# Raw weight pieces loaded across stages, and q and k loaded five steps ahead in place of nine

## The chip, the core and the metric

The kernel runs on one core of a Trainium2 chip. The metric is the device time of one execution in microseconds (us); the time of a kernel is the median of several runs.

## The reference

Talking-heads attention on 8 batches of 12 heads, 448 positions and 64 dimensions, followed by a Fourier mix and a feed-forward layer. Everything is float32 except the two weight matrices, which come as float64.

```python
scores = scale * np.matmul(q, k.transpose(0, 1, 3, 2))
scores = np.einsum('bhij,hg->bgij', scores, w_pre)      # mix the heads
scores = scores - np.max(scores, axis=-1, keepdims=True)
attn = np.exp(scores)
attn = attn / (np.sum(attn, axis=-1, keepdims=True) + 1e-09)
attn = np.einsum('bhij,hg->bgij', attn, w_post)         # mix them again
x = np.matmul(attn, v)                                  # -> (8, 448, 768)
# ...
X = np.fft.fft(np.fft.fft(x, axis=1), axis=2)
u = x + np.real(X)
un = (u - mu) / np.sqrt(var + 1e-06)
out = u + np.maximum(un @ w_ch1, 0.0) @ w_ch2
```

## The kernel before

It has two phases. The mix phase does attention and the Fourier mix and stores u; the feed-forward phase reads u back and multiplies by both weight matrices in a scheme with seven products for eight. The mix phase is a software pipeline of 192 steps, 24 for each batch (`GS = 24`, `TOT = 192`). The order of instructions on TensorE (PE), VectorE (DVE), ScalarE (ACT) and GpSimd (POOL) is fixed by the program; each engine works its list in order. One step is this:

```python
while s < TOT or any(fill.values()):
    old = len(later)
    n = take("none", s)                  # loads that are due: q, k, v
    if 0 <= s + LM < TOT:
        emit_premix(s + LM)              # PE L449, LM = 2 steps ahead
    flush()
    if 0 <= s < TOT:
        emit_postmix(s)                  # PE L486, needs the scaled PP of step s
    if 0 <= s + LM < TOT:
        emit_max(s + LM)                 # DVE L457
        emit_exp(s + LM)                 # ACT L465
    take("AV", s)                        # PE L513
    if 0 <= s < TOT:
        emit_turn(s)                     # DVE L497, one a step
    if s >= 4:
        wts.deal(1)                      # one DVE operation of the weights' work
    take("QK", s)                        # PE L423
    # ... gather of step s + 4 on SP (Kr <- Sb)
    if 0 <= s + LM < TOT:
        emit_scale(s + LM)               # POOL L476, two instructions
    for _ in range(old):
        later.pop(0)()
    for _ in range(min(len(folds), 1 if n and s > 3 else 2)):
        folds.pop(0)()                   # POOL L567 to L588
    take("full", s)                      # transposes (L400, L546), emit_z (L611), emit_s2 (L627)
    s += 1
```

q and k of the next batch come in six tiles, in the order k0, q0, q2, k1, q1, k2; each is loaded in two halves, in two steps, with two DMAs that POOL issues (batch 0's are issued by SP and ACT). There are four buffers for them. The tile is transposed at its step `a`, and its load is due nine steps before, unless the buffer rule (`old`) puts it later:

```python
old = loads[-4] + 2 if len(loads) > 3 else -99
loads.append(f + a - GS)
for y in range(2):
    due("none", max(old, f + a - GS - 9) + y,
        lambda b=b, xx=xx, nm=nm, y=y: emit_load_qk(b, xx, nm, y))
# ...
for pr in range(3):
    due("none", f + AT_AV[-1][pr] + 2, lambda b=b, pr=pr: emit_load_v(b, pr))
```

The Fourier mix along the positions works on folded operands. A pair of row groups brings 8 folds on POOL, and the second pair of a batch 4 more (`both`, L588), which write `xf`, the operand of TensorE's L611. emit_z takes whatever folds are still open:

```python
def emit_z(b, par, y):
    while ("xf", par) not in batches[b] or folds:
        folds.pop(0)()
    # ... 4 matmuls on st["xf", par] (L611)
```

The weights' work turns the float64 matrices into float32 tiles and their sums, on DVE, between the other work. A stage is four raw pieces of 7 DVE operations each, then four sums, then a store; in the mix phase there are five stages, dealt one DVE operation a step from step 4 on, and 25 more in the feed-forward phase. There one stage is added at a time, and ended before the next block (`wts.deal(1000)`).

```python
def add(self, c, n):
    ps, sums, w, dst = self._parts(c)[n]
    raws, box = {}, {}

    def load(k):
        if k < len(ps):
            src, f, _ = ps[k]
            raws[k] = self.praw.tile([P, DH, 2], U32, name="raw64", tag="raw64")
            nc.gpsimd.dma_start(out=raws[k][:, :f, :].rearrange("p f w -> p (f w)"),
                                in_=src.bitcast(U32))

    def begin(k):
        # ...
        load(k + self.ahead)             # ahead = 1 in the mix phase, 2 after it
        raw = raws.pop(k)
        # ...
        vec.tensor_scalar(box["tmp"].bitcast(U32), box["hi"], 0x7fffffff, None,
                          op0=ALU.bitwise_and)     # L218
    # ...
    self.ops.append((lambda: [load(k) for k in range(self.ahead)], False))
```

Of the kernel before, what the change touches and what calls it, by code (L numbers as in the profile page):

```python
# [11 lines left out]
U32 = mybir.dt.uint32  # L12
# [4 lines left out]
P = 128  # L17
# [20 lines left out]
GS = NG * GT  # L38
# [24 lines left out]
DH = DM // 2  # L63
# [68 lines left out]
def _f32(bits: int) -> float:  # L132
    return float(np.array(bits, np.uint32).view(np.float32))
# [11 lines left out]
class _Weights:  # L145
# [7 lines left out]
    def __init__(self, nc, w_ch1, w_ch2, scr):  # L153
        self.nc = nc
        self.w_ch1, self.w_ch2 = w_ch1, w_ch2
        self.w1 = [scr.tile([7, P, NK, FC], F32, name=f"w1_{c}") for c in range(NC)]
        self.w2 = [scr.tile([7, P, FM, DH], F32, name=f"w2_{c}") for c in range(NC)]
        self.ops = []

    def open(self, ctx, tc, ahead=1):  # L160
        self.ahead = ahead
# [29 lines left out]
    def add(self, c, n):  # L191

        nc, vec = self.nc, self.nc.vector
        ps, sums, w, dst = self._parts(c)[n]
        raws, box = {}, {}

        def load(k):
            if k < len(ps):
                src, f, _ = ps[k]
                raws[k] = self.praw.tile([P, DH, 2], U32, name="raw64", tag="raw64")  # L200
                nc.gpsimd.dma_start(  # L201
                    out=raws[k][:, :f, :].rearrange("p f w -> p (f w)"),
                    in_=src.bitcast(U32))

        def begin(k):
            _, f, slot = ps[k]  # L210
            if k == 0:
                box["st"] = self.pst.tile([P, 7, DH], F32, name="wst", tag="wst")
            load(k + self.ahead)
            raw = raws.pop(k)
            box["lo"], box["hi"] = raw[:, :f, 0], raw[:, :f, 1]
            box["tmp"] = self.ptmp.tile([P, DH], F32, name="tmp", tag="tmp")[:, :f]
            box["top"] = box["st"][:, slot, :f]
            vec.tensor_scalar(box["tmp"].bitcast(U32), box["hi"], 0x7fffffff, None,  # L218
                              op0=ALU.bitwise_and)

        def clamp():
            vec.tensor_scalar(box["tmp"], box["tmp"], _f32(0x38000000),
                              _f32(0x47efffff), op0=ALU.max, op1=ALU.min)

        def shift():
            vec.tensor_scalar(box["top"].bitcast(U32), box["tmp"].bitcast(U32),
                              0x07ffffff, 3, op0=ALU.bitwise_and,
                              op1=ALU.logical_shift_left)

        def sign():  # L230
            top = box["top"].bitcast(U32)
            vec.scalar_tensor_tensor(top, box["hi"], 0xc0000000, top,
                                     op0=ALU.bitwise_and, op1=ALU.bitwise_or)

        def power():
            vec.tensor_scalar(box["tmp"].bitcast(U32), box["top"].bitcast(U32),
                              0xff800000, None, op0=ALU.bitwise_and)

        def lower():
            vec.scalar_tensor_tensor(box["tmp"], box["lo"], 2.0 ** -52, box["tmp"],  # L240
                                     op0=ALU.mult, op1=ALU.mult)

        def whole():
            vec.tensor_tensor(box["top"], box["top"], box["tmp"], op=ALU.add)

        def total(o, a, op, b):
            st = box["st"]
            vec.tensor_tensor(st[:, o, :w], st[:, a, :w], st[:, b, :w], op=op)

        def store():  # L250
            nc.gpsimd.dma_start(out=dst.rearrange("k p f -> p k f"),
                                in_=box["st"][:, :, :w])

        self.ops.append((lambda: [load(k) for k in range(self.ahead)], False))
        for k in range(len(ps)):
            self.ops.append((lambda k=k: begin(k), True))
            for fn in (clamp, shift, sign, power, lower, whole):
                self.ops.append((fn, True))
        for a in sums:
            self.ops.append((lambda a=a: total(*a), True))  # L260
        self.ops.append((store, False))
# [10 lines left out]
def mix_phase(ctx, tc, ident, q, k, v, w_pre, w_post, u_scr, u_rev, wts):  # L272
# [4 lines left out]
    nc = tc.nc  # L277
# [85 lines left out]
    def emit_load_qk(b, xx, nm, y):  # L363

        src = q if nm == "q" else k
        if y == 0:
            batches[b]["raw" + nm, xx] = praw.tile([P, C7, 2, D], F32, name="raw" + nm,
                                                   tag="raw")
        t = batches[b]["raw" + nm, xx]
        for x in range(2):  # L370
            eng = nc.gpsimd if b else (nc.sync, nc.scalar)[x]
            eng.dma_start(
                out=t[64 * y:64 * y + 64, :, x, :],
                in_=src[b, 6 * y + 2 * xx + x].rearrange("(p c) d -> p c d", c=C7))

    def emit_load_v(b, pr):
        t = pvv.tile([P, 2, C7 * D], F32, name="vv", tag=f"vv{pr}")
        for y in range(2):
            h = 6 * y + 2 * pr
            nc.gpsimd.dma_start(  # L380
                out=t[64 * y:64 * y + 64, :, :],
                in_=v[b, h:h + 2].rearrange("h (p c) d -> p h (c d)", c=C7))
        batches[b]["v", pr] = t


    def emit_xpose(b, xx, nm):
        st = batches[b]
        raw = st.pop(("raw" + nm, xx))
        w = WQ if nm == "q" else S
        t = pqt.tile([P, 2, w], F32, name=nm + "T", tag=nm + "T")  # L390
        st[nm + "T", xx] = t
        rt = _row(t)
        if nm == "q":
            nc.gpsimd.memset(t[:, :, 0:MG], 0.0)
            nc.gpsimd.memset(t[:, :, MG + S:WQ], 0.0)
        evs = []
        for c0, n in ((0, 4), (4, 3)):
            ps = ms_tile()
            for c in range(n):
                nc.tensor.transpose(  # L400
                    ps[:, c * P:(c + 1) * P],
                    raw[:, c0 + c].rearrange("p x d -> p (x d)"), ident[:, :])
            if nm == "q":
                dst = _ap(t, MG + c0, [[rt, P], [1, n], [WQ, 2], [C7, 64]])
                src = ps[:, :n * P].rearrange("p (c y t) -> p c y t", c=n, y=2)
            else:
                dst = _ap(t, 32 * c0, [[rt, P], [32, n], [HS, 4], [1, 32]])
                src = ps[:, :n * P].rearrange("p (c y t) -> p c y t", c=n, y=4)
            evs.append(lambda dst=dst, src=src, n=n: copy(ENG["tr", nm, n], dst, src))
        return evs  # L410
# [255 lines left out]
    def due(kind, at, fn):  # L666
        fill[kind].append((at, len(fill[kind]), fn))
# [5 lines left out]
    for b in range(B):  # L673
        f = b * GS
        at_t = [(a, nm, xx) for xx, at in enumerate(AT_T) for nm, a in zip("qk", at)]
        for a, nm, xx in sorted(at_t, key=lambda e: e[0]):
            old = loads[-4] + 2 if len(loads) > 3 else -99
            loads.append(f + a - GS)
            for y in range(2):
                due("none", max(old, f + a - GS - 9) + y,  # L680
                    lambda b=b, xx=xx, nm=nm, y=y: emit_load_qk(b, xx, nm, y))
        for xx, at in enumerate(AT_T):
            for nm, a in zip("qk", at):
                due("full", f + a - GS, lambda b=b, xx=xx, nm=nm: emit_xpose(b, xx, nm))
        for pr in range(3):
            due("none", f + AT_AV[-1][pr] + 2, lambda b=b, pr=pr: emit_load_v(b, pr))
        for n in range(2 * NG):
            for xx in range(3):
                due("QK", f + BS * n - 7 + AT_QK[n][xx],
                    lambda n=2 * NG * b + n, xx=xx: (emit_qk(n, xx), n))  # L690
        for n in range(NG):
            g = groups[b * NG + n]
            for pr in range(3):
                due("AV", f + GT * (n + 1) + AT_AV[n][pr],
                    lambda g=g, pr=pr: (emit_av(g, pr), None))
            due("full", f + AT_X[n], lambda g=g: emit_x(g))
        for n, at in enumerate(AT_Z):
            due("full", f + at, lambda b=b, n=n: emit_z(b, n // 2, n % 2))
        for pair in range(2):
            for par in range(2):  # L700
                due("full", f + AT_S[pair][par],
                    lambda b=b, pair=pair, par=par: emit_s2(b, pair, par))
# [23 lines left out]
    with tc.manual_schedule(engines={ET.PE, ET.DVE, ET.Activation, ET.Pool}):  # L726
        while s < TOT or any(fill.values()):
            old = len(later)
            n = take("none", s)
# [323 lines left out]
```

## Time and profile before

| | |
|---|---|
| time, median of 3 runs | 2538.48 us (2532.35 to 2538.54) |
| span of the profiled execution | 2531.2 us |
| PE busy | 2402.8 us, 95% |
| PEld (weight loads, beside PE) | 1547.6 us, 61% |
| DVE busy | 1519.4 us, 60% |
| ACT busy | 789.8 us, 31% |
| POOL busy | 694.8 us, 27% |
| DMA moved | 372.05 MB, mean 147 GB/s |
| HBM read and written | 211.98 and 74.34 MB |
| chain that ended last | PE 82%, DMA 6%, DVE 5%, ACT 4%, POOL 1%, issue 1% |

The page of a profile gives busy times, the span in 40 slices of about 63 us with the busy share of each engine in tenths, the chain of work that ended last, and groups of instructions by line. "L218" is line 218 of the kernel. "raw" in the trace is the weights' raw piece, "rawq" and "rawk" are q and k, "vv" is v. A bracket at the end of a line of the timeline, as in `[4.58 <-DMA raw]`, is the idle time of that engine just before the instruction, and what ended it. A line of the waits gives total us, the number of times, and the longest.

### The profile page before, as it was taken

Reading aid. Unit: us, or ns where it says so; the run is one execution under the profiler, and the core shown is the slowest. Engines: PE = TensorE matmul, PEld = TensorE weight load, DVE = VectorE, ACT = ScalarE, POOL = GpSimd, SP = SyncE. Lnnn points to the kernel's source line nnn. Section 1 sums busy time; section 2 is a strip of 40 time slices with the busy share of each in tenths; the row PEclk is TensorE's granted clock in tenths of the full one; section 3 lists DMA queues with packets and bytes.
Section 4 is the critical chain, followed back from the end, with each engine's and each line's share of the span. In section 5 each row is a group of like instructions: output and inputs, shape, how many; then the busy total and the mean of one; then the engine's idle time right before and its main releaser. Section 6 shows DMA issues by size and latency. Waiting matters only on the chain.

```text
span 2531.2 us, 47914 instructions
## 1 busy us (share of the span) xinstructions
PE 2402.8 (95%) x18608; PEld 1547.6 (61%) x18608; DVE 1519.4 (60%) x3103; ACT 789.8 (31%) x2059; POOL 694.8 (27%) x1112
## 2 busy tenths in 40 slices
PE   6799999989999976999999999999999999999999
PEld 2344444444444445777777777777777777777776
DVE  3667687777778645777466646664666466633333
ACT  3566566656556632232111111111111111111110
POOL 2565767666666651111000000000000000000000
PEclk9999999999999997999999999999999999999999
DMA  5554546455454445633544444444444444343331
GB/s 127 158 152 143 165 149 168 146 172 154 158 162 156 135 167 158 218 130 140 205 130 152 144 153 132 152 144 152 132 152 144 152 133 152 131 151 118 131 112 50
DMA packets 165311, 372.05 MB, mean 147 GB/s; under 512 B 33854, under 2 KB 87126, under 8 KB 165086
## 3 DMA queue, kind: packets, MB, share of 16 engines
q1 hardware_dynamic: 129038, 260.22, 31.0%
q0 software_dynamic: 30480, 107.39, 14.3%
q8 instruction: 149, 2.44, 0.4%
q10 hardware_dynamic: 5568, 1.38, 0.3%
q14 instruction: 76, 0.62, 0.1%
HBM read 211.98 MB, written 74.34 MB: 113 GB/s over the span
## 4 chain that ended last, share of the span: by engine, by line
PE 82%; DMA 6%; DVE 5%; ACT 4%; POOL 1%; issue 1%; SPq 1%; ACTq 0%; POOLq 0%; DVEq 0%
PE psP L894 17%; PE psP L948 17%; PE psR L894 9%; PE psR L948 9%; PE mx L449 6%; PE ms L513 5%; PE psQ L948 4%; PE psQ L894 4%; PE po L486 4%; DMA Kr<-Sb 4%; PE ms L423 3%; ACT PP L465 3%; DVE nmx L457 3%; PE ms L627 1%; PE ms L611 1%
## 5 line engine op out<-in xcount | busy, mean ns | idle before, releaser
L894 PE MATMUL psP<-ub,w1t 128*128 128x256 f32 x2016 | 463.6, 379 | 0.0
L948 PE MATMUL psP<-w2t,h 128*128 128x384 f32 x1344 | 460.9, 486 | 0.0
L894 PEld LDWEIGHTS psP<-ub,w1t 128*128 128x128 f32 x2016 | 383.4, 190 | 60.7
L948 PEld LDWEIGHTS psP<-w2t,h 128*128 128x128 f32 x1344 | 254.4, 190 | 165.9
L201 POOL DMA_DIRECT2D raw<-in_moe_w_ch_dram x120 | 69.7, 581 | 987.7 <-DVE tmp L240 969.8
L465 ACT ACTIVATE PP<-mx,nmx 128x448 f32<-128x448 f32 x384 | 240.3, 631 | 314.1 <-DVE nmx L457 287.5
L476 POOL TENSOR_SCALAR PP<-PP,rcp 128x448 f32<-128x448 f32 x384 | 241.3, 639 | 334.7 <-DVE rcp L474 259.7
L457 DVE TENSOR_REDUCE nmx<-mx 128x1 f32<-128x448 f32 x384 | 221.5, 619 | 141.8 <-PE mx L449 131.8
L449 PE MATMUL mx<-Kr,kw 60*64 60x448 f32 x1536 | 216.3, 566 | 57.8 <-ACT PP L465 44.5
L954 DVE TENSOR_TENSOR u<-u,psP 128x384 f32<-128x384 f32 x336 | 183.4, 553 | 142.7 <-PE psP L948 140.6
L899 ACT COPY h<-psP 128x512 f32<-128x512 f32 x42 | 24.7, 587 | 761.7 <-PE psP L894 761.7
L894 PE MATMUL psR<-ub,w1t 128*128 128x256 f32 x1008 | 231.4, 379 | 0.0
L948 PE MATMUL psR<-w2t,h 128*128 128x384 f32 x672 | 230.5, 486 | 0.0
L497 DVE STREAM_TRANSPOSE Pv<-po 128x896 f32<-128x896 f32 x192 | 212.6, 1108 | 7.8 <-PE po L486 7.6
L894 PEld LDWEIGHTS psR<-ub,w1t 128*128 128x128 f32 x1008 | 191.4, 190 | 26.3 <-DVE ub L873 0.3
L905 DVE TENSOR_TENSOR h<-h,psQ 128x512 f32<-128x512 f32 x42 | 28.9, 688 | 295.0 <-PE psQ L894 295.0
L423 PE MATMUL ms<-kT,qT 64*60 64x448 f32 (+1 forms) x1536 | 193.9, 564 | 5.5 <-DVE qT L305 5.5
L486 PE MATMUL po<-PP,kw 60*32 60x448 f32 x3072 | 193.1, 560 | 0.0
L305 ACT COPY Sb<-ms 124x448 f32<-124x448 f32 x384 | 184.8, 541 | 18.3 <-DMA Kr<-Sb 12.5
L513 PEld LDWEIGHTS ms<-Pv,vv 64*64 64x64 f32 x5376 | 144.0, 133 | 73.0 <-issue 31.7
L948 PEld LDWEIGHTS psR<-w2t,h 128*128 128x128 f32 x672 | 127.2, 190 | 87.4
L513 PE MATMUL ms<-Pv,vv 64*64 64x120 f32 x5376 | 167.8, 268 | 1.8 <-issue 1.7
(92 smaller groups left out, 2667.5 us busy)
## 6 DMA issues: line engine op xcount, KB each, us to landing
ub<-ub SPq DMA_DIRECT2D x294, 384.0 KB
Kr<-Sb SPq DMA_DIRECT2D x768, 105.0 KB
raw<-in_moe_w_ch_dram POOLq DMA_DIRECT2D x72, 256.0 KB, 3.2
raw<-in_moe_w_ch_dram POOLq DMA_DIRECT2D x48, 384.0 KB, 3.4
w<-wst POOLq DMA_DIRECT2D x18, 896.0 KB, 4.9
w<-wst POOLq DMA_DIRECT2D x12, 1344.0 KB, 5.8
w1t<-w SPq DMA_DIRECT2D x42, 384.0 KB
w2t<-w SPq DMA_DIRECT2D x42, 384.0 KB
```

Of the source, the lines that this page charges most:

```text
L305: (nc.scalar.copy if eng == "a" else nc.vector.tensor_copy)(out=out, in_=in_)
L423: nc.tensor.matmul(pss[x][64 * y:64 * y + r0 + 64 - lo, :S], st["qT", xx][64 * x:64 * x + 64, y, lo:r0 + 64], st["kT", xx][64 * x:64 * x + ...
L449: nc.tensor.matmul(mx[64 * z:64 * z + 64, x, :S], kw1[64 * x:64 * x + KR, :], Kr[64 * x:64 * x + KR, z, :], start=True, stop=True)
L457: nc.vector.tensor_reduce(nmx[:, x:x + 1], steps[T]["mx"][:, x, :S], axis=AX.X, op=ALU.max, negate=True)
L465: nc.scalar.activation(PP[:, x, :], steps[T]["mx"][:, x, :S], ACTF.Exp, bias=steps[T]["nmx"][:, x:x + 1], accum_out=den[:, x:x + 1])
L476: nc.gpsimd.tensor_scalar(PP[:, x, :], PP[:, x, :], rcp[:, x:x + 1], 1.0, op0=ALU.mult, op1=ALU.mult)
L486: nc.tensor.matmul(po[o:o + 32, z, :S], kw2[64 * z:64 * z + KR, y, :], PP[64 * z:64 * z + KR, :, c * HS:(c + 1) * HS], start=True, stop=True)
L497: nc.vector.transpose(g["Pv"][:, T % GT, :].rearrange("p (z s) -> p z s", z=2), steps[T]["po"][:, :, :S])
L513: nc.tensor.matmul(pss[y][64 * x:64 * x + 64, :nu * R], st["v", pr][64 * y:64 * y + 64, x, jb * D:(jb + 1) * D], _ap(Pv, 64 * y * rp + 32 ...
L894: nc.tensor.matmul(p[:, m, :], w1[i][:, kc, m * P:(m + 1) * P], ub[:, kc, :], start=i in OPENS and m == kc == 0, stop=kc == NK - 1, skip_g ...
L948: nc.tensor.matmul(p, lhs[i][:, kf, x * P:(x + 1) * P], w2[i][:, kf, :], start=i in OPENS and kf == 0, stop=kf == FM - 1, skip_group_check ...
L954: nc.vector.tensor_tensor(us_, us_, p, op=ALU.add)
```

## The change

The first part keeps one list of raw pieces for all stages, so that the load of the piece `ahead` of the one in work also reaches into the next stage, where before a stage's first piece was loaded only when the stage began. It is meant to spare DVE the wait for that piece. The second part loads q and k five steps ahead of their transposes in place of nine, so that they meet v's loads less.

```diff
-        self.ops = []
+        self.ops, self.pieces, self.raws = [], [], {}
...
         ps, sums, w, dst = self._parts(c)[n]
-        raws, box = {}, {}
-
-        def load(k):
-            if k < len(ps):
-                src, f, _ = ps[k]
-                raws[k] = self.praw.tile([P, DH, 2], U32, name="raw64", tag="raw64")
-                nc.gpsimd.dma_start(
-                    out=raws[k][:, :f, :].rearrange("p f w -> p (f w)"),
-                    in_=src.bitcast(U32))
+        box, k0 = {}, len(self.pieces)
+        self.pieces.extend(ps)
+
+        def load(n):
+
+            for k in range(len(self.raws), min(n + 1, len(self.pieces))):
+                src, f, _ = self.pieces[k]
+                raw = self.raws[k] = self.praw.tile([P, DH, 2], U32, name="raw64",
+                                                    tag="raw64")
+                nc.gpsimd.dma_start(out=raw[:, :f, :].rearrange("p f w -> p (f w)"),
+                                    in_=src.bitcast(U32))
...
-            load(k + self.ahead)
-            raw = raws.pop(k)
+            load(k0 + k + self.ahead)
+            raw = self.raws[k0 + k]
...
-        self.ops.append((lambda: [load(k) for k in range(self.ahead)], False))
+        self.ops.append((lambda: load(k0 + self.ahead - 1), False))
...
             for y in range(2):
-                due("none", max(old, f + a - GS - 9) + y,
+                due("none", max(old, f + a - GS - 5) + y,
                     lambda b=b, xx=xx, nm=nm, y=y: emit_load_qk(b, xx, nm, y))
```

## Prediction

> **What bounds the kernel now.** I read the page first, then the chain in order of time, the waits, the timeline, and a table by windows. Part 2 of the page splits the span:
>
> ```profile
> PE   6799999989999976999999999999999999999999
> DMA  5554546455454445633544444444444444343331
> ```
>
> From slice 17 on (about 990 us) TensorE is full: that is the feed-forward phase, 1540 us long. There the changed kernel issues the same instructions (each stage of weights is added and drained within its block, so nothing can be loaded across stages). All that can move lies in the mix phase, 0 to 990 us. It runs in 192 steps, 24 for each of 8 batches, and the starts of the 192 transposes of L497 in the timeline cut it into steps. An undisturbed step takes 3.79 us, with TensorE's groups back to back, so this phase is TensorE-bound too and loses time only where TensorE, which works in program order, is held up. I write "step 12 of batch 1" for the one 12 after that batch's first.
>
> Two kinds of hold-up stand out. First, the waits name a DVE wait for the weights' raw pieces, one for each of the 5 stages:
>
> ```profile
> DVE tmp L218 <- DMA raw<-in_moe_w_ch_dram: 35.5, 5, 14.2
> PE ms L611 <- POOL xf L588: 10.4, 2, 10.2
> ```
>
> They start at 73.9 (14.25 us), 210.0 (4.58), 359.7 (2.64), 511.1 (7.67) and 662.5 (6.40). The second line matters later: it is what TensorE does when L611's operand is not folded yet, at the end of the phase, where nothing covers it. The stall at 210 in the timeline:
>
> ```profile
> 203.97 0.59 POOL L201 DMA_DIRECT2D raw<-in_moe_w_ch_dram  x1
> ...
> 209.99 0.29 DVE L218 TENSOR_SCALAR tmp<-raw 128x256 uint32<-128x256 uint32 x1 [4.58 <-DMA raw<-in_moe_w_ch_dram]
> ...
> 211.59 0.98 PE L423 MATMUL ms<-kT,qT 64*64 64x448 f32 x8 [2.17 <-DVE qT L305]
> ...
> 214.01 1.77 PE L449 MATMUL mx<-Kr,kw 60*64 60x448 f32 x8 [1.44 <-ACT PP L465]
> ```
>
> The load goes out one step before its use and lands 6 us later; DVE blocks, TensorE idles, and its next group runs at 1.77 us in place of 0.98.
>
> Second, steps 4 to 6 of most batches are long. The windows of batch 3 (columns: window, its length, busy time of PE, PEld, DVE, ACT, POOL, then clock, DMA share, GB/s):
>
> ```profile
> 379.40:383.40 4.00, 4.00 (x96) 2.12 (x92) 3.17 (x7) 2.85 (x10) 3.89 (x7) 1.00 0.29 101
> 383.40:387.40 4.00, 4.00 (x96) 2.15 (x91) 2.79 (x7) 2.94 (x10) 3.96 (x7) 1.00 0.59 168
> 387.40:391.60 4.20, 4.20 (x92) 2.33 (x88) 2.77 (x7) 2.91 (x10) 4.16 (x8) 1.00 0.86 216
> 391.60:397.30 5.70, 4.44 (x36) 0.94 (x32) 2.79 (x7) 2.20 (x6) 5.70 (x11) 1.00 1.00 208
> 397.30:405.40 8.10, 5.21 (x54) 2.74 (x53) 4.81 (x11) 3.07 (x8) 3.65 (x6) 1.00 0.87 200
> ```
>
> k loads, then v and q loads together, fill the DMA engines, and the gathers of Sb into Kr come late: the chain shows "Kr<-Sb" for 13.29 us from 396.48, and only 4.64 us from 844.48 in the last batch, which loads v but no q or k.
>
> **What the Trainium skill says.** *Trainium Kernel Development and Optimization*, Key Constraints: DMAs from the SP, ACT and POOL queues run on the same 16 DMA engines and interleave. Agrees: SP's gathers stretch while POOL's loads hold the share at 0.86 to 1.00. *GPSIMD Engine Reference*, 3.1: about 2.6 cycles an element for two inputs, which at its 1.2 GHz makes 0.83 us for 385; the trace has 1.00 us for each L588, dispatch included. *TensorE: Matmul & The Clock Gate*, Part 1: after an idle window of about 3.4 us the array runs at half clock until it has been busy as long. Agrees in size: 1.77 against 0.98 us after the stall above.
>
> **The change, part by part.** The order of instructions on PE and DVE is the same in both builds; ACT and SP differ by one load's place in the prologue. Only POOL is reordered.
>
> (a) Raw pieces across stages. A stage's first piece now goes out with the last piece of the stage before, 11 steps ahead of use. Four DVE waits vanish; the first stage's load keeps its place. Worth in step times: batch 1, steps 12 and 13 take 8.12 and 5.04 against 3.97 and 3.95 elsewhere, 5.2; batch 5, 9.99, 5.15 and 5.94 against 3.97, 3.95 and 5.2, 8.0 (I use 7.8); batch 2 step 20, 7.14 against 5.07, 2.1; batch 4 step 4, 10.38 against about 6.9 in other congested batches, 3.5. Sum -18.6 us.
>
> (b) q and k four steps later. Before, of a batch's six tiles k0 goes out at steps 1 and 2, q0 at 3 and 4, q2 at 5 and 6, k1 at 7 and 8, against v at 3, 4, 5. After, those four go out at 5 to 12 (q1 and k2 stay at 12 to 15, held by the buffer rule), so v shares a step with k0 only, at step 5. Steps 3 to 7 sum to 24.49, 29.55, 29.56, 31.14, 27.33 and 29.21 in batches 1 to 6, and 24.46 in batch 7. Batch 1 lacks the two L627 groups (1.3 us each) that the later ones have in those steps, so with v alone I expect 21.9 there. Excess over v alone: 2.6, 5.1, 5.1, 6.7 less the 3.5 counted above, 2.9, 4.8: 23.7. With k0 still on the third v load I take 14 of it. The moved loads now meet the gathers at steps 9 to 12: +3. In batch 0 the first raw piece sits behind 0.45 MB of q on the same queue; some 2.4 MB drained in the 19.5 us from 54.4 to 73.9, 0.12 MB a us, so its landing comes 3.7 us earlier: -4.
>
> (c) What moves with them. The code runs two folds a step on POOL, but only one when a load was due (`1 if n and s > 3 else 2`). Before, the 12 folds of a pair's end had steps 9 to 11 free of loads and were done at the end of step 14, one a step at the close; the z matmuls (L611) found xf ready:
>
> ```profile
> 434.42 1.00 POOL L588 TENSOR_TENSOR xf<-xq 113x385 f32<-113x385 f32 x1
> 435.38 1.53 POOL L372 DMA_DIRECT2D rawq<-in_q_dram  x2
> 436.94 1.26 POOL L476 TENSOR_SCALAR PP<-PP,rcp 128x448 f32<-128x448 f32 x2
> 438.17 1.16 POOL L588 TENSOR_TENSOR xf<-xq 113x385 f32<-113x385 f32 x1
> ```
>
> and TensorE's L611 begins at 440.92. After, every one of steps 5 to 15 has a load, only 9 folds run, the ninth being the first L588, and emit_z forces the last three at step 14: all four L588 stand together on POOL behind the scaling (L476) of that step. z needs the first two. For batch 2, from the L476 at 306.96 to 308.21, with 1.46 for a pair of loads, 1.0 for a fold, 1.35 for an L581/L582 group, 1.26 for an L476 pair, 1.2 for the indirect store, 0.6 for a raw load: fold, loads, raw 3.06 to 311.3, L476 to 312.56; store, group, loads 4.06, L476 to 317.9; fold, loads 2.46, but its operand comes at 319.4 and the sum is at 320.4, L476 to 321.65; fold, two pairs 3.9, L476 to 326.85; fold, loads, memsets 2.55, L476 to 330.7; group, loads 2.81, L476 to 334.75; two L588, 336.75. TensorE would be at L611 at 328.8: it waits 8 us. The same sum gives 8.1 in batch 1, 8.1 in 3, 6.7 in 4, 8.5 in 5 and 7.2 in 6 (the last batch's z, after the loads end, is unchanged): 46.7. Nothing covers it, since TensorE is the bound, and each wait is past the clock's window: a slow group or two after it, 0.8 and 0.6 us as at 214, +1.4 each, 8.4.
>
> Sum: -18.6 - 14 + 3 - 4 + 46.7 + 8.4 = +21.5. On 2538.5 that is 2560; since the POOL sum takes every wait at its worst, I take 5 off: 2555 us.
>
> **Rivals.** (1) The change does as meant and z hardly waits: POOL would have to be ahead of TensorE by more than 5 us at step 14. For: POOL is busy only 27% of the span. Against: in batches 2, 3 and 6 its L476 already starts 2.4 us after its operand there. Time: 2538 - 34, about 2505. (2) z waits only for the chain through the L476 before it (5.1 to 5.9 us, no POOL backlog), and the loads are fully relieved (-24): -18.6 - 24 - 4 + 6 x 6.9 = -5, about 2533. (3) The load waits merely move, k0 under the third v load being as bad as q was: +35, about 2573.
>
> **Range and chances.** The stage waits are nearly certain, the z wait is certain in kind and 5 to 8.5 us in size, the relief the least sure. 8 in 10: 2526 to 2577. 2% is 51 us; faster by that needs no z wait at all (0.03), slower needs it to exceed the sum without any relief (0.05); within, 0.92.
>
> **What would show it.** Waits: DVE L218 for raw falls from five to one, about 10 us; L611 waits for POOL L588 in six more places, 5 to 9 us each. Steps 13 to 15 of batches 1 to 6 grow, 12 and 13 of batches 1 and 5 shrink to about 4, steps 4 to 6 shrink by some 2. The feed-forward phase keeps its length. I am wrong if L611 shows no wait, if the phase ends before 985 us, or if steps 4 to 6 are unchanged.

## The result, and the profile after

The changed kernel takes 2552.06 us, median of 4 runs (2546.21 to 2554.03), against 2537.32 before (2532.35 to 2538.54): a ratio of 1.0058, 95% interval 1.0036 to 1.008. It is slower by about 15 us, inside the predicted range and 3 us from the predicted 2555.

In the page's slices of the changed kernel, TensorE's row and the DMA engines' row:

```profile
PE   6899998979898985999999999999999999999999
DMA  4544546363544545544444444444444444343331
```

From the end of the mix phase on nothing changed: from the last of the 192 transposes (L499 in the changed kernel, two lines below its place before) to the end are 1606.5 us, against 1606.9. In the mix phase TensorE's row now has an 8 or a 7 again and again, about one a batch, where it had 9s. The waits (total us, times, longest) answer to the two lines shown of before. L613 is the matmul L611 of before, and PEld its weight loads:

```profile
PEld ms L613 <- POOL xf L590: 48.7, 14, 10.5
PE ms L613 <- POOL xf L590: 41.3, 14, 10.2
...
DVE tmp L220 <- DMA raw<-in_moe_w_ch_dram: 11.8, 1, 11.8
```

TensorE's wait at L613 grew from 10.4 us in 2 waits to 41.3 in 14, two more in each of six batches: 30.9 us, 5.2 a batch. DVE's five waits for a raw piece became one.

The timeline of batch 2 at step 14 shows the place. POOL and PE, in order of time:

```profile
324.55 0.98 PE L425 MATMUL ms<-kT,qT 64*64 64x448 f32 x8
...
327.72 1.26 POOL L478 TENSOR_SCALAR PP<-PP,rcp 128x448 f32<-128x448 f32 x2
328.95 3.85 POOL L590 TENSOR_TENSOR xf<-xq 113x385 f32<-113x385 f32 x4
329.99 0.69 PE L613 MATMUL ms<-ts,xf 113*97 113x113 f32 x2 [4.46 <-POOL xf L590]
330.94 2.94 PE L613 MATMUL ms<-ts,xf 112*97 112x112 f32 x14 [0.26 <-POOL xf L590]
333.67 1.70 PE L402 MATMUL ms<-ident,rawq 128*128 128x128 f32 x7
335.30 1.64 PE L451 MATMUL mx<-Kr,kw 60*64 60x448 f32 x8
```

TensorE ends L425 at 325.5 and has nothing to do until POOL has scaled (L478) and done the first of four folds in a row (L590). After that L402 and L451 take 1.7 and 1.6 us where the same groups take 0.98 undisturbed. The windows around it (columns as in the windows of batch 3: the clock is the third number from the end) say why:

```profile
319.50:325.50 6.00, 5.94 (x102) 2.55 (x96) 4.16 (x8) 3.44 (x11) 5.93 (x12) 1.00 0.74 187
325.50:330.00 4.50, 0.04 (x5) 0.01 (x1) 1.38 (x4) 1.71 (x6) 4.46 (x8) 0.98 0.60 179
330.00:336.90 6.90, 6.64 (x35) 4.75 (x35) 1.08 (x1) 1.92 (x3) 4.30 (x7) 0.52 0.22 72
336.90:341.90 5.00, 5.00 (x112) 2.41 (x110) 3.61 (x8) 2.84 (x10) 1.26 (x2) 1.00 0.23 86
```

The wait itself costs 4.5 us; then the granted clock is 0.52 for 6.9 us.

The relief that the change was meant to bring is there too. Batch 3, steps 2 to 5, after, the same steps as the last four windows shown of before:

```profile
386.60:390.70 4.10, 4.10 (x100) 2.25 (x96) 2.92 (x8) 2.95 (x10) 1.90 (x3) 1.00 0.33 125
390.70:394.80 4.10, 4.10 (x91) 2.02 (x80) 2.80 (x7) 2.92 (x10) 3.20 (x7) 1.00 0.84 228
394.80:398.60 3.80, 2.80 (x36) 0.74 (x32) 2.65 (x8) 2.20 (x6) 2.25 (x5) 1.00 0.85 225
398.60:404.80 6.20, 5.30 (x62) 2.90 (x58) 4.69 (x12) 3.07 (x8) 4.89 (x8) 1.00 0.86 221
```

Steps 4 and 5 take 3.8 and 6.2 us in place of 5.7 and 8.1, and the chain has the gather "Kr<-Sb" here for 4.20 us (from 397.17) in place of 13.29.

With the starts of the 192 transposes in each timeline, the difference to the kernel before can be put down to steps. Sums over all 8 batches, us; "total" is at the last transpose, so it also holds the differences before the first one and in steps 0 to 2 (4.5 us in steps 0 to 2 of late_dist4, 11.3 in those of late_dist4_old_raws):

| kernel | steps 3-7 | 8-11 | 12-13 | 14 | 15-19 | 20-23 | total |
|---|---|---|---|---|---|---|---|
| the changed kernel | -27.9 | +0.3 | +1.6 | +46.1 | 0.0 | -1.1 | +18.8 |
| raw_alone | +4.2 | 0.0 | -9.1 | -0.4 | 0.0 | -1.5 | -6.8 |
| qk_alone | -25.1 | +0.3 | +10.4 | +48.6 | +0.2 | -0.9 | +34.2 |
| after_old_pace | -26.3 | +3.5 | +5.3 | +0.8 | 0.0 | -2.1 | -17.7 |
| before_new_pace | +0.1 | -0.1 | +1.0 | +39.4 | +1.3 | -1.1 | +41.6 |
| late_stages | -41.5 | +4.0 | -1.6 | +2.7 | +1.1 | -6.9 | -41.3 |
| early_doubles | -29.3 | +5.4 | +1.8 | +3.4 | +1.5 | -8.4 | -26.4 |
| later_z | -24.4 | +0.1 | +1.1 | -6.7 | +15.7 | -0.3 | -12.0 |
| dist4 | -28.9 | +3.3 | -2.9 | -0.3 | +6.2 | -7.9 | -30.7 |
| late_dist4 | -44.5 | +4.8 | -8.4 | -0.5 | +8.0 | -2.7 | -38.1 |
| late_dist4_old_raws | -47.4 | +4.8 | -8.4 | -0.4 | +16.2 | -3.7 | -26.8 |

The changed kernel's row holds nearly all of it: 28 us gained in steps 3 to 7, 46 lost in step 14. In six batches step 14 went from 5.1 to 6.2 us to 12.4 to 14.1. The profile of the kernel before is of an execution of 2533.17 us, some 4 us under its median, so the totals lie above the differences of the medians (14.7 us for the changed kernel).

### The profile page after: what moved, and what is told of

It reads as the page before. It is cut to its first block, busy times and chain, and to the rows that moved or that the text cites. A ratio compares the mean times of both kernels' runs of the same rounds, so it can differ in the third digit from the quotient of the medians.

```text
span 2549.6 us, 47913 instructions
## 1 busy us (share of the span) xinstructions
PE 2404.3 (94%) x18608; PEld 1557.3 (61%) x18608; DVE 1513.6 (59%) x3103; ACT 791.8 (31%) x2059; POOL 695.8 (27%) x1112
## 4 chain that ended last, share of the span: by engine, by line
PE 82%; POOL 5%; ACT 4%; DVE 4%; DMA 3%; issue 2%; SPq 1%; ACTq 0%; POOLq 0%; DVEq 0%
PE psP L896 17%; PE psP L950 17%; PE psR L896 9%; PE psR L950 9%; PE mx L451 6%; PE ms L515 5%; PE psQ L950 4%; PE psQ L896 4%; PE po L488 4%; PE ms L425 3%; ACT PP L467 3%; DMA Kr<-Sb 3%; DVE nmx L459 2%; PE ms L613 1%; PE ms L629 1%
## 5 line engine op out<-in xcount | busy, mean ns | idle before, releaser
L478 POOL TENSOR_SCALAR PP<-PP,rcp 128x448 f32<-128x448 f32 x384 | 242.4, 642 | 355.9 <-DVE rcp L476 280.9
L451 PE MATMUL mx<-Kr,kw 60*64 60x448 f32 x1536 | 211.4, 566 | 51.8 <-ACT PP L467 39.8
L499 DVE STREAM_TRANSPOSE Pv<-po 128x896 f32<-128x896 f32 x192 | 212.7, 1108 | 6.7 <-PE po L488 6.7
L896 PEld LDWEIGHTS psR<-ub,w1t 128*128 128x128 f32 x1008 | 191.4, 190 | 26.3 <-DVE ub L875 0.3
L907 DVE TENSOR_TENSOR h<-h,psQ 128x512 f32<-128x512 f32 x42 | 28.9, 688 | 295.5 <-PE psQ L896 295.5
L488 PE MATMUL po<-PP,kw 60*32 60x448 f32 x3072 | 191.0, 554 | 0.0
L425 PE MATMUL ms<-kT,qT 64*60 64x448 f32 (+1 forms) x1536 | 189.7, 556 | 0.0
```

Of the source, the lines that this page charges most:

```text
L425: nc.tensor.matmul(pss[x][64 * y:64 * y + r0 + 64 - lo, :S], st["qT", xx][64 * x:64 * x + 64, y, lo:r0 + 64], st["kT", xx][64 * x:64 * x + ...
L451: nc.tensor.matmul(mx[64 * z:64 * z + 64, x, :S], kw1[64 * x:64 * x + KR, :], Kr[64 * x:64 * x + KR, z, :], start=True, stop=True)
L478: nc.gpsimd.tensor_scalar(PP[:, x, :], PP[:, x, :], rcp[:, x:x + 1], 1.0, op0=ALU.mult, op1=ALU.mult)
L488: nc.tensor.matmul(po[o:o + 32, z, :S], kw2[64 * z:64 * z + KR, y, :], PP[64 * z:64 * z + KR, :, c * HS:(c + 1) * HS], start=True, stop=True)
L499: nc.vector.transpose(g["Pv"][:, T % GT, :].rearrange("p (z s) -> p z s", z=2), steps[T]["po"][:, :, :S])
L896: nc.tensor.matmul(p[:, m, :], w1[i][:, kc, m * P:(m + 1) * P], ub[:, kc, :], start=i in OPENS and m == kc == 0, stop=kc == NK - 1, skip_g ...
```

## The experiments

Each ratio below is against runs of the kernel before on the same chip. My theory T was that the loss comes from the pace of the folds, which the moved loads set through `1 if n and s > 3 else 2`. Rival R1: the raw pieces cost. Rival R2: the moved loads cost by their own place on POOL and the DMA engines, whatever the folds do. The first four kernels take the change apart.

**raw_alone.** The changed kernel with q and k put back.

```diff
-                due("none", max(old, f + a - GS - 5) + y,
+                due("none", max(old, f + a - GS - 9) + y,
```

> The raw pieces are loaded across stages, q and k stay nine steps ahead. Theory T (the loss comes from the fold pacing, which this kernel does not touch): faster than before, 2537 - 6 to 2537 - 19, about 2524; L611 waits for L588 only at the end of the phase (10 us, as before). Within it two views of batch 5, where the changed kernel's step 13 lasts 10.6 us: if the stage's store alone delays the gathers there, steps 12 and 13 of batch 5 still sum to about 15; if it takes the k loads beside it, they sum to 8 to 10 here. Rival R1 (raw pieces are what costs): 2537 or slower.

2525.64 us against 2538.05: ratio 0.9956 (0.994 to 0.9973). The raw part alone is a gain, so R1 falls. (Its +4.2 us in steps 3 to 7, in batches 1, 5 and 7, I did not trace.) L613 waits 10.2 us at the end only, as before. Steps 12 and 13 of batch 5 sum to 9.3 us, so the store alone does not make the changed kernel's step of 10.6 us. The moved loads and the store do not make it by themselves either: in after_old_pace, which has both at the same steps, the two steps sum to 11.5 us in place of 14.7. But batch 4 gained only 0.7 in its steps 3 to 7: its step 4 fell from 10.4 to 4.2 and its step 5 rose from 6.5 to 10.8. There the DVE's wait of 7.7 us had only stood in front of a wait for the gathers, here in raw_alone and then in the changed kernel:

```profile
508.26 0.97 ACT L307 COPY Sb<-ms 124x448 f32<-124x448 f32 x2 [4.17 <-DMA Kr<-Sb]
508.85 0.98 PE L548 MATMUL ms<-ident,XT 128*113 128x128 f32 x3 [3.76 <-ACT Sb L307]
```

```profile
515.84 0.55 DVE L642 TENSOR_TENSOR X<-X,ms 113x383 f32<-113x383 f32 x1
515.86 1.45 POOL L374 DMA_DIRECT2D rawk<-in_k_dram  x2
520.63 0.97 ACT L307 COPY Sb<-ms 124x448 f32<-124x448 f32 x2 [6.79 <-DMA Kr<-Sb]
521.22 0.98 PE L548 MATMUL ms<-ident,XT 128*113 128x128 f32 x3 [6.49 <-ACT Sb L307]
```

ACT writes Sb only when the gather out of it has landed, and TensorE waits behind ACT. In batch 5 the changed kernel's gather is late as well:

```profile
676.15 2.67 PE L451 MATMUL mx<-Kr,kw 60*64 60x448 f32 x6 [3.56 <-DMA Kr<-Sb]
678.75 1.74 PE L488 MATMUL po<-PP,kw 60*32 60x448 f32 x16
```

**qk_alone.** The kernel before with the one number changed.

```diff
-                due("none", max(old, f + a - GS - 9) + y,
+                due("none", max(old, f + a - GS - 5) + y,
```

> q and k five steps ahead, raw pieces as before. Theory T: slower than before: 46 us more in step 14 of batches 1 to 6, less some 5 where DVE's stage wait lets POOL catch up (batches 1 and 5), 20 to 26 us less in steps 3 to 7, so +12 to +25, about 2555; L611 waits for L588 in six more places. Rival R1 (raw pieces are what costs): 2537 - 26 = 2511. Rival R2 (the moved loads' place on POOL and on the DMA engines costs, whatever the folds do): also slower, told apart by the next run.

2567.01 us: ratio 1.0113 (1.0095 to 1.013), so all of the loss is in this half, and it is larger by itself than with the other half beside it, and larger than I expected. L611 waits 40.7 us in 14 times, as in the changed kernel. Steps 12 and 13 grew by 10.4 us, of which 4.1 in batch 5: there DVE waits 10.5 us for the raw piece, in place of 6.4.

**after_old_pace.** The changed kernel, with the folds at the steps where the kernel before has them.

```diff
-            for _ in range(min(len(folds), 1 if n and s > 3 else 2)):
+            m_ = s % GS
+            one = s > 3 and (3 <= m_ <= 5 or s < TOT - GS
+                             and (m_ in range(1, 9) or m_ in range(12, 16)))
+            for _ in range(min(len(folds), 1 if one else 2)):
```

> The changed kernel, with the folds at the steps where the kernel before has them (one at batch steps 1 to 8 and 12 to 15, two at 9 to 11), so that only the loads move. Theory T: L611 finds xf ready, step 14 of batches 1 to 6 falls from about 13.2 to 5.2 (-46); POOL now has two folds and a pair of loads in steps 9 to 11 and comes late by up to 2 us a batch (+0 to +15): 2506 to 2520. Rival R2 (the loads' place itself costs): step 14 stays long, 2545 to 2552.

2516.36 us: ratio 0.9916 (0.9899 to 0.9933). The wait at L613 is gone but for the one at the end:

```profile
PEld po L488 <- POOL PP L478: 55.7, 59, 3.4
...
PE po L488 <- POOL PP L478: 12.6, 8, 2.6
...
PE ms L613 <- POOL xf L590: 10.5, 2, 10.3
```

Step 14 is back (+0.8), and R2 falls: with all loads where the change puts them, the kernel is faster than both. The first two lines are the part that I expected of POOL running late. In most of the 59 waits of the weight loads TensorE still has matmuls to do; in eight it is idle itself, 12.6 us, where the changed kernel has no such wait. They stand in steps 12 and 13 of batches 1 to 6, and steps 8 to 13 are longer by 8.8 us in all.

**before_new_pace.** The kernel before, loads and raw pieces untouched, with the changed kernel's pace.

```diff
-            for _ in range(min(len(folds), 1 if n and s > 3 else 2)):
+            m_ = s % GS
+            one = s > 3 and (3 <= m_ <= 5 or s < TOT - GS and m_ in range(3, 16))
+            for _ in range(min(len(folds), 1 if one else 2)):
```

> The kernel before, its loads and raw pieces untouched, with the folds at the pace of the changed kernel (one a step in batch steps 3 to 15, the last three forced by emit_z). Theory T: step 14 of batches 1 to 6 grows by 5 to 8 us each (less in 1 and 5, where DVE's stage wait lets POOL catch up), 2537 + 30 to 45, about 2575; L611 waits for L588 in six more places. Rival R2: no wait, 2537.

2574.36 us: ratio 1.0145 (1.0132 to 1.0158). The loss appears with no load moved at all, in the same step:

```profile
340.85 3.84 POOL L588 TENSOR_TENSOR xf<-xq 113x385 f32<-113x385 f32 x4
...
341.88 0.69 PE L611 MATMUL ms<-ts,xf 113*97 113x113 f32 x2 [3.86 <-POOL xf L588]
```

These two runs together show it both ways: by the steps, the pace without the loads costs 42 us, and the change without the pace gains 18 (by the medians 36 and 22).

The other six ask what else the steps show, and whether a faster version follows.

**late_stages.** after_old_pace, with the weights' work begun later.

```diff
-            if s >= 4:
+            if s >= 16:
                 wts.deal(1)
```

> The changed kernel with the old fold pace, and the weights' work begun at step 16 in place of step 4, so that the first raw piece no longer queues behind the tables and v, and the stages' stores fall on steps 0 and 8 to 16 of a batch, away from v's loads. If the stores and the first load meet v's loads on the DMA engines (my view of batches 0 and 4): step 4 of batch 0 falls from 13.7 to about 4, step 5 of batch 4 from 11.7 to about 6, together -15 on the 2516 of the old pace: about 2501. If DVE's waits there only hide other waits for the gathers: -3 at most, about 2513.

2495.07 us against 2531.63: ratio 0.9856 (0.9836 to 0.9876). Steps 3 to 7 gained 15.2 us more than with the old pace alone (-41.5 against -26.3), 6.2 of it in batch 4 and 4.5 in batch 0, where DVE's wait for the first raw piece fell from 11.0 to 2.1 us. Batch 0 gained less than the 10 expected: its step 4 fell to 6.0, but steps 5 and 6 rose to 7.7 and 5.8, where v and the tables are still loaded beside the gathers; that they are the cause was not tested apart.

**early_doubles.** The changed kernel, two folds at steps 6 to 8.

```diff
-            for _ in range(min(len(folds), 1 if n and s > 3 else 2)):
+            m_ = s % GS
+            one = s > 3 and (3 <= m_ <= 5 or s < TOT - GS
+                             and m_ in (1, 2, 3, 4, 5, *range(9, 16)))
+            for _ in range(min(len(folds), 1 if one else 2)):
```

> The changed kernel with two folds a step at batch steps 6 to 8 in place of 9 to 11, the number ready at step 12 being the same. If the 2 us by which steps 12 and 13 are still long with the old pace come from POOL running late behind two folds, a store and two pairs of loads in steps 9 to 12: 2516 - 6 to - 10, about 2508. If POOL is overloaded anyway in steps 6 to 14, the delay only moves to steps 8 to 11: 2513 to 2519.

2512.94 us, ratio 0.9931 (0.9913 to 0.995), which overlaps the old pace's interval. Steps 8 to 13 sum to +7.2 in place of +8.8: the lateness mostly moved to earlier steps. That is what the second figure says, though 1.6 us of the 8.8 did go.

**later_z.** The changed kernel and its own pace, with z and what hangs on it later.

```diff
-AT_Z = (38, 38, 41, 41)
-AT_S = ((40, 44), (53, 55))
+AT_Z = (41, 41, 42, 42)
+AT_S = ((42, 45), (53, 55))
```

> The changed kernel with its own fold pace, and z (L611 of the kernel before) three steps later, the products after it two steps and one step later. Theory T (what counts is the distance from the second L588 to z, here two steps as in the kernel before): the 46 us of step 14 go, POOL has one fold a step: 2552 - 46 to - 52, about 2503, below the old pace's 2516. If the products and stores that hang on z then hold up others instead: 2515 to 2535.

2519.44 us, ratio 0.9952 (0.9935 to 0.9968). L613 again waits only at the end (10.2 us), so the distance from fold to z is what counts, as T says; but of my two figures the second held: the z groups now stand in steps 17 and 18 and the products in steps 18 and 21. The work moved there from steps 14, 16 and 20, and steps 14 to 23 are 8.7 us longer in all than before (-6.7 + 15.7 - 0.3). The cause of that I did not separate.

**dist4.** after_old_pace, with q and k four steps ahead.

```diff
-                due("none", max(old, f + a - GS - 5) + y,
+                due("none", max(old, f + a - GS - 4) + y,
```

> The changed kernel with the old fold pace, q and k four steps ahead: no load of k shares a step with one of v. If the rest of the gathers' delay in steps 5 to 7 (about 2 us a batch above the last batch's quiet steps) comes from k0 meeting the third v load: -6 to -10; two pairs of loads now stand on POOL in steps 12 to 15 beside L588 and make po late: +3 to +10. Sum 2510 to 2520, no clear gain.

2502.62 us, ratio 0.9886 (0.9867 to 0.9904), against the old pace's 0.9916: a small gain whose intervals touch, and not where I expected most of it. Steps 3 to 7 gained 2.6 us, steps 12 and 13 gained 8.1 (k1 moved there from steps 11 and 12, yet TensorE's waits of L488 for the scaling fell in them from 12.6 to 6.7 us), steps 15 to 19 lost 6.2 (3.9 of it are waits of L488 for the scaling, of which the old pace has none there). In this run, in late_stages and in early_doubles, steps 20 to 23 were 5 to 6 us shorter over the eight batches than with the old pace; no edit touches those steps in all three. All three ran on one chip, on which the kernel before took 2531.63 us in place of 2538.05; late_dist4, on another chip, has -2.7 there, near the old pace's -2.1. The chip may be the cause; this was not tested. The ratios, each against the same chip, do not depend on it.

**late_dist4.** The edits of late_stages and dist4 together.

> The changed kernel with the old fold pace, the weights' work begun at step 16, and q and k four steps ahead. The two gains act at different steps (batches 0 and 4 for the stages, steps 5 to 7 and 13 of each batch for the distance), so the ratios 0.9856 and 0.9886 against the old pace's 0.9916 should nearly multiply: 0.983 of before, about 2490. If both only remove the same waits for the gathers: 0.9856.

2493.85 us against 2538.69: ratio 0.9822 (0.9804 to 0.9841). As expected (0.983), it has the lowest ratio of all and beats both kernels, by 1.8% the one before. Its interval still meets that of late_stages (from 0.9836 on), so what dist4 adds to late_stages is near the noise.

**late_dist4_old_raws.** The same with the weights' class as in the kernel before, so that a stage's first piece is loaded when the stage begins.

> The same with the raw pieces loaded stage by stage, as in the kernel before. The stages now begin where POOL's queue on the DMA engines is short, so DVE waits 2 to 5 us at each of four starts and the raw part is worth 6 to 15 us: ratio 0.986 to 0.989. If the raw part is worth nothing once the stages are moved (its load lands in time by itself): 0.983, as its partner.

2507.76 us: ratio 0.9883 (0.9863 to 0.9903). DVE's waits for raw pieces, here and in late_dist4, from the two lists of waits:

```profile
DVE tmp L218 <- DMA raw<-in_moe_w_ch_dram: 22.7, 5, 7.6
```

```profile
DVE tmp L220 <- DMA raw<-in_moe_w_ch_dram: 2.4, 1, 2.4
```

The raw part takes 20.3 us of DVE's wait away and 11 to 14 us of the time (26.8 against 38.1 by the steps, 2507.76 against 2493.85 by the medians). The ratio is inside the expected range, but it comes from two waits only. In batch 4 (a wait of 7.6 us at step 16) steps 15 to 19 are 6.7 us longer than in late_dist4, and in batch 6 (6.3 us at step 0) steps 0 to 2 are 6.5 longer: there the wait costs about its length. The waits of 4.4 us (batch 2, step 0) and 2.0 us (batch 3, step 8) cost 0.4 us and nothing; in batch 2 those steps are 4.1 us longer than before in late_dist4 as well, without that wait.

## Why the prediction was right, point by point

**The feed-forward phase** kept its length, within 0.4 us.

**(c), the folds.** Right in mechanism and nearly in size. All four L588 (now L590) stand together behind the scaling in six batches. Predicted 46.7 us of waits and 8.4 of slow clock, 55.1; measured +46.1 in step 14. The split was wrong in both terms: TensorE waited 30.9 us at L613 in place of 46.7, and the other 15.2 us, 2.5 a batch in place of 1.4, go with the slow clock. Of batch 2's 8.2 us more in step 14, 4.7 are waits; the rest follows them, in 6.9 us at a clock of 0.52. (The fold's price in the sum was the trace's 1.00 us, and the four L590 of batch 2 took 3.85; the 0.83 us that the prediction has beside it is only an estimate.)

The wait was shorter than in my sum for two reasons. The sum waited for two folds, but TensorE began z after the first and then waited only 0.26 us for the second, as the two lines of L613 above show. And my sum let TensorE reach z on time, but the gathers had held it up: steps 12 and 13 of batches 2, 3, 4 and 6 grew by 2.3, 0.7, 0.9 and 1.5 us, and in each of these batches the weight loads of L451 wait there for Kr (0.9 to 1.9 us; before, none but 0.1 us in batch 6). In batch 2:

```profile
317.26 0.19 PEld L451 LDWEIGHTS mx<-Kr,kw 60*64 60x64 f32 x4 [0.85 <-DMA Kr<-Sb]
...
322.74 0.19 PEld L451 LDWEIGHTS mx<-Kr,kw 60*64 60x64 f32 x2 [0.84 <-DMA Kr<-Sb]
```

In batch 5, where step 13 lasted 10.6 us, the wait at z was 3.2 us in place of 8.5.

**(a), the raw pieces.** The waits fell from five to one, as said, but the sum of -18.6 was too large beside the rest of the change. Alone this half is worth 12.4 us by the medians and 6.8 by the profiled steps. Batch 1 gave 3.9 in steps 12 and 13 against 5.2; batch 4 gave 0.7 in place of 3.5; batch 5 gave 5.8 alone, and in the changed kernel 0.4 in place of 7.8, with k and the store behind the same wait. The failing step is the reading of "10.38 against about 6.9": I took the rest of that step as the load's price, but it was a wait in front of another.

**(b), q and k.** The relief was mis-sized the other way. The predicted -14 became -20.9 in steps 3 to 7 of batches 1 to 6 in qk_alone. The predicted +3, for moved loads that meet the gathers in steps 9 to 12, came one step later and larger: steps 8 to 11 stay at +0.3, and in the changed kernel steps 12 and 13 of batches 2, 3, 4 and 6 have the 5.4 us named above. I had assumed that k0 on the third v load would keep some 10 of the 23.7; under 3 us of it stayed. In batch 0 DVE's wait fell by 2.4 us, from 14.2 to 11.8, not 3.7, and the sum of its steps 3 to 7 by 1.1 in place of 4 (3.3 in qk_alone).

**The sum.** -18.6 - 14 + 3 - 4 + 46.7 + 8.4 gave +21.5, and 5 off for waits at their worst gave 2555; the profile's total is +18.8. The raw part alone fell short by 11.8 us (6.8 by the steps for 18.6). Against it stood the larger relief, by 6.9 us, and a smaller cost of z, by 9.0. That errors of this size nearly cancelled, and the sum came within 3 us, is luck; what held is the mechanism of the largest term and, within a sixth, its size.

**The rivals.** (1) needed POOL to be ahead of TensorE by more than 5 us at step 14; it was not. (2) is near what each part did: a z wait of about 5 us and full relief. It failed on the clock (2.5 us a batch where it had 1.4) and on the raw part. (3) failed: the load waits did not merely move to k0.

## What to carry to other kernels

A rule in the program that looks at one thing and acts on another ties them: here the number of loads due set the pace of the folds, and moving loads by four steps starved the folds. When a change moves work, list what is paced by it, and count the steps from each producer to its consumer on the engines in order. Before taking a wait away, look what would have been late just behind it: of the 7.7 us that DVE waited in batch 4, 0.7 came back.

## What the runs showed of the hardware that I had not expected

A TensorE wait of 4.5 us is followed by 6.9 us at a granted clock of 0.52. Each of the six waits at z has one such stretch beside it, about 6.8 us at a clock of 0.50, part of which can lie in the wait itself. Over the six, 30.9 us of waits made step 14 longer by 46.1, so such a wait cost about half its own length again; I had allowed 1.4 us each, read off two slow groups.

And POOL's 27% is an average over the whole span, and in the feed-forward phase it is nearly idle: in the window of batch 2 just before the wait it was busy for 5.93 of 6.00 us. The issue of one q load keeps it 0.73 us (the pair 1.46), more than one scaling instruction of 0.64 us. In after_old_pace this made TensorE itself idle for 12.6 us, in eight waits of L488 for the scaling.
